# Attention in two-step blocks, one pool for all PSUM banks, and a new order of a linear-attention and feed-forward kernel

## The chip, the cores and the metric

The kernel runs on one core of a Trainium2 chip. The metric is the time of one execution on the device in microseconds (us); the smaller, the better. A core has a matrix engine (TensorE, PE in the profile, with its weight loads as PEld), a vector engine (VectorE, DVE), a scalar engine (ScalarE, ACT), GpSimd (POOL) and SyncE (SP). Each runs its own queue of instructions in order, and waits on semaphores for the others. In this kernel TensorE's results go to PSUM, in eight banks of up to 128 x 512 values of 32 bit; VectorE and ScalarE read them there. Loads and stores are DMA transfers that POOL, SP and ACT issue.

## The reference

Two parts, one after the other. First, a linear attention with decay for 4 batches and 8 heads, 768 positions, head size 64. In blocks of positions it is

```python
intra = einsum('bhic,bhjc->bhij', qb, kb) * Dmask     # lam ** (i - j) for i >= j, else 0
intra = einsum('bhij,bhjd->bhid', intra, vb)
inter = einsum('bhid,bhde->bhie', qb * lam_pow, kv_state)
out[:, :, sl] = intra + inter
kv_state = lam_block * kv_state + einsum('bhsd,bhse->bhde', kb * rev_pow, vb)
```

Then the result, as 3072 tokens of 512 values, goes through two matrix products with ELU between them:

```python
h = x @ w_in                                          # 512 x 2048
g = where(h > 0, h, exp(min(h, 0)) - 1)
out = g @ w_out                                       # 2048 x 512
```

The kernel may work with another block length (it uses 128), because the state carries the rest.

## The kernel before, in words

A **step** is 128 positions of one batch, all eight heads: 24 steps, step `s` being chunk `s // 4` of batch `s % 4`. The state of a batch (`sbd`, two copies used in turn) goes from a step to the one four later. Steps 0 to 3 have no state yet, so for them the part with the state is left out.

The attention of one step is made of these helpers. `load_step` (L73) issues three loads on POOL, of k and q into `kq` and of v into `vt`, cast to 16 bit on the way. `att_TK`, `att_TQ` and `att_T` (L205 to L227) transpose k and q on TensorE into PSUM and copy them out, with ScalarE or VectorE as their last arguments say; `att_D` (L229) lets a DMA do it instead, issued on SP, from step 8 on. `att_V` (L236) makes three products on VectorE: q times the decay (`qs`), v times the decay (`vd`), the old state times the decay (`sd`). `att_S` (L281) multiplies k and q into two banks `psS` and then multiplies these by the decay mask into `P`, on VectorE (L297). `att_U` (L258) multiplies k and `vd` into `psU`, and VectorE adds `sd` to give the new state (L275, L279). `att_O` (L301) multiplies P and v, and qs and the state, into `psO` (L323, L331), and ScalarE copies that to `xt` (L336), the input of the feed-forward part.

The feed-forward part is cut into quarters. `mm1(s, u)` (L346) makes one bank `psH` of the first product; ScalarE takes its exponential `e` (L359) and its positive part `r` (L364; with `relu=1` VectorE makes r, L362). `finish_g` (L367) joins the oldest pending e and r to `g` on VectorE (L376). From step 4 on two steps share an `mm1`, so a pair has eight of them (u = 0 to 7), of 256 columns. `mm2(s, i)` (L383) adds a quarter of the second product into `psM`; after i = 3 ScalarE copies the bank (L403) and SP stores it (L404). The weights `wi` and `wo` come in four blocks of 512 KB each (as stored), also issued by POOL.

Nothing is scheduled by a planner: the order of the calls in the kernel is the order on every engine. It is a long list written out by hand (L416 to L517), in which attention and feed-forward of steps 0 to 3 are mixed, and then a loop over pairs (L521): p = 4, 6, ..., 22. In the loop the attention of step p + 2 stands ahead of u = 0 and that of p + 3 ahead of u = 4, each with the `att_S` of the step after it; each u has one `mm1` of the pair and one `mm2` taken from the list `late`, in which the two steps of the pair alternate. At the start, `warm` (L409) puts matmuls of zeros between the first pieces.

PSUM is split by tags: psT one bank, psM two, psU one, psS two, psH two. A tile waits until the tile that last held its bank has been read.

What sets the order of loads is POOL's list (L107 to L127), in which block 1 of `wi` comes first, then step 1, then blocks 0 and 2 and so on. Step 0 comes by SP and ACT as 32 bit (`k32`, `q32`, `v32`) and is cast by VectorE (L418, L420) and ScalarE (L427).

Of the kernel before, what the change touches and what calls it, by code (L numbers as in the profile page):

```python
# [11 lines left out]
ALU = mybir.AluOpType  # L12
# [3 lines left out]
def kernel(  # L16
# [23 lines left out]
    NBV = 5  # L40
    SEP = 2
# [66 lines left out]
    load_step(0)  # L108
    load_wi(1)
    load_step(1)  # L110
    clear(sbd[2][1])
    clear(sbd[1][1])
    load_wi(0)
    load_wi(2)
    load_step(2)
    load_wi(3)
    clear(sbd[3][0])
    load_step(3)
    clear(sbd[0][1])
    clear(sbd[2][0])  # L120
    load_wo(0)
# [3 lines left out]
    clear(sbd[1][0])  # L125
    clear(sbd[3][1])
    load_step(4)  # L127
# [48 lines left out]
    def mask_arg(hh):  # L176
        for hp in range(NHP):
            h = 2 * hp + hh
            nc.vector.scalar_tensor_tensor(
                out=mask[:, hh, hp, :], in0=ijf[:], scalar=loglam[:, h : h + 1],  # L180
                in1=negm[:], op0=ALU.mult, op1=ALU.add,
            )
# [15 lines left out]

    def copy(e, out, in_):
        if e:  # L200
            nc.scalar.copy(out=out, in_=in_)
        else:
            nc.vector.tensor_copy(out, in_)

    def att_TK(s, e=1):  # L205
        psK = ps.tile([128, NHP, 128], FP16, tag="psT", name=f"psK{s}")
        transposes(psK[:], s, 0)
        t = asb.tile([128, NHP, 128], FP16, tag="kT", bufs=3, name=f"kT{s}")
        st[s]["kT"] = t[:]
        copy(e, t[:], psK[:])  # L210

    def att_TQ(s, e=0):

        psQ = ps.tile([128, NHP, 128], FP16, tag="psM", bufs=2, name=f"psQ{s}")
        transposes(psQ[:], s, 1)
        t = asb.tile([128, NHP, 128], FP16, tag="qT", bufs=3, name=f"qT{s}")
        st[s]["qT"] = t[:]
        copy(e, t[:], psQ[:])

    def att_T(s, ke=1, qe=0):  # L220
        psT = ps.tile([128, 2, NHP, 128], FP16, tag="psT", name=f"psT{s}")
        transposes(psT[:, 0], s, 0)
        transposes(psT[:, 1], s, 1)
        for i, (n, e) in enumerate((("kT", ke), ("qT", qe))):
            t = asb.tile([128, NHP, 128], FP16, tag=n, bufs=3, name=f"{n}{s}")
# [3 lines left out]
    def att_D(s):  # L229
        t = asb.tile([128, 2 * NHP, 128], FP16, tag="kqT", bufs=3, name=f"kqT{s}")  # L230
# [5 lines left out]
    def att_V(s):  # L236
# [3 lines left out]
        if c:  # L240
            d["qs"] = asb.tile([128, NHP, 128], FP16, tag="qs", bufs=2, name=f"qs{s}")
# [3 lines left out]
        d["vd"] = asb.tile([128, H, 64], FP16, tag="vd", bufs=2, name=f"vd{s}")  # L245
# [5 lines left out]
        if c:  # L251
            d["sd"] = asb.tile([128, NHP, 128], FP32, tag="sd", bufs=2, name=f"sd{s}")
# [5 lines left out]
    def att_U(s):  # L258
# [4 lines left out]
        psU = ps.tile([128, NHP, 64], FP32, tag="psU", name=f"psU{s}")  # L263
# [7 lines left out]
        new = sbd[b][c % 2]  # L271
# [9 lines left out]
    def att_S(s):  # L281
# [3 lines left out]
            ps.tile([128, NHP, 128], FP32, tag="psS", bufs=2, name=f"psS{s}_{hh}")  # L285
            for hh in range(2)
# [8 lines left out]
        d["P"] = asb.tile([128, 2, NHP, 128], FP16, tag="P", bufs=2, name=f"P{s}")  # L295
        for hh in range(2):
            nc.vector.tensor_tensor(  # L297
                out=d["P"][:, hh], in0=psS[hh][:], in1=mask[:, hh], op=ALU.mult
            )

    def att_O(s):  # L301
# [5 lines left out]
        elif s % 2 == 0:  # L307

            xt[s] = asb.tile([128, NHP, 2 * L], FP16, tag="xt2", bufs=3, name=f"xt{s}")
        else:  # L310
            xt[s] = xt[s - 1]
        x = 0 if s < ONE else s % 2

        if s < SEP:
            psO = ps.tile([128, NHP, 128], FP32, tag="psM", bufs=2, name=f"psO{s}")
        elif s == B:
            psO = ps.tile([128, NHP, 128], FP32, tag="psU", name=f"psO{s}")
        else:
            psO = ps.tile([128, NHP, 128], FP32, tag="psT", name=f"psO{s}")
# [16 lines left out]
        nc.scalar.copy(out=xt[s][:, :, x * L : (x + 1) * L], in_=psO[:])  # L336
# [9 lines left out]
    def mm1(s, u, relu=0):  # L346
        w = 1 if s < ONE else 2
        nt = NQ // w
        psH = ps.tile([128, nt, w * L], FP32, tag="psH", bufs=2, name=f"psH{s}_{u}")
# [8 lines left out]
        e = msb.tile([128, nt, w * L], FP32, tag="e", bufs=4, name=f"e{s}_{u}")  # L358
        nc.scalar.activation(e[:], psH[:], AF.Exp)  # L359
        r = msb.tile([128, nt, w * L], FP16, tag="r", bufs=4, name=f"r{s}_{u}")  # L360
# [46 lines left out]
    warm_ps = ps.tile([128, 512], FP32, tag="psH", bufs=2, name="warm")  # L407
# [7 lines left out]

    warm(13)  # L416
    mask_arg(0)
    nc.vector.tensor_copy(kq[0][:, 1], q32[:])  # L418
    att_TQ(0)
    nc.vector.tensor_copy(kq[0][:, 0], k32[:])  # L420
    warm(4)
    mask_exp(0)
    att_TK(0)
    mask_arg(1)
    mask_exp(1)
    warm(3)
    nc.scalar.copy(out=vt[0][:], in_=v32[:])  # L427
    att_S(0)
    att_V(0)
    warm(4)  # L430
    att_O(0)
    att_TK(1)
    att_U(0)
    att_V(1)
    mm1(0, 1, 1)
    att_TQ(1, 1)
    finish_g()
    att_S(1)
    mm1(0, 0, 1)
    att_O(1)  # L440
    finish_g()
    mm1(0, 2)
    mm1(1, 1)
    att_TQ(2, 0)
    load_step(5)
    att_V(2)
    finish_g()
# [128 lines left out]
```

## Time and profile before

| | |
|---|---|
| runs, median (lowest to highest) | 218.79 us (218.54 to 219.06), 3 runs |
| the profiled execution's own time | 218.84 us |
| its span | 217.0 us |
| PE, DVE, ACT, POOL busy | 206.8, 152.5, 137.9, 70.8 us |
| DMA | 24.84 MB, 13.24 MB of it through POOL's queue |
| granted TensorE clock | 1.00 |

The span is what the profiler saw of the engines; the execution's own time has 1.84 us around it. "Busy" sums the time of an engine's instructions. A matmul that waits for its operands can count as busy, so that PE's share says little about how much it computes: `mm1` of a pair needs 0.87 us for 8 matmuls and `mm2` 0.86 us for 4 where they follow each other without a wait. In the chain of waits each row is a start, a duration and what ran or was waited for; it follows the work that ended last back to its cause. The windows give busy time in us and instructions (x) for PE, PEld, DVE, ACT and POOL, then granted clock, busy share of the DMA engines and GB/s.

### The profile page before, as it was taken

The page shows a single profiled execution, that of the slowest core. Times are in us where ns is not written, and L with a number is a line of the kernel's source. Part 1 is how long each engine was busy: PE and PEld are TensorE (multiplying, and loading weights), DVE is VectorE, ACT ScalarE, POOL GpSimd, SP SyncE. Part 2 cuts the span into 40 slices and gives each one's busy share as a digit, 9 for nine tenths or more (in the row PEclk, how much of TensorE's full clock was granted, in tenths as well). Part 3 has the DMA queues.
Part 4 walks back from the last instruction along what each step waited for, and adds up shares of the span by engine and source line. Part 5 has one row for each costly group of instructions (what it writes and reads, how often), then busy time and mean ns, then how long its engine had stood idle before and what let it go on. Part 6 is the DMA issues. An engine that isn't in the chain of part 4 may idle for free.

```text
span 217.0 us, 5089 instructions
## 1 busy us (share of the span) xinstructions
PE 206.8 (95%) x2072; PEld 138.9 (64%) x2072; DVE 152.5 (70%) x266; ACT 137.9 (64%) x263; POOL 70.8 (33%) x90
## 2 busy tenths in 40 slices
PE   7778699999999999999999999999999999999993
PEld 2368576765666766766676676676676666666651
DVE  4785983899878868868868778778775464533440
ACT  3737564956755765865855855855955955866851
POOL 8875833865341242242242242144000000000000
PEclk9999999999999999999999999999999999999999
DMA  4999999999995994996995993999680320200202
GB/s 102 193 200 181 183 206 176 154 211 141 164 198 38 128 182 31 135 165 42 139 171 37 147 169 26 152 172 69 105 112 0 76 73 2 100 0 0 100 0 97
DMA packets 99767, 24.84 MB, mean 114 GB/s; under 512 B 92448, under 2 KB 96800, under 8 KB 99744
## 3 DMA queue, kind: packets, MB, share of 16 engines
q0 software_dynamic: 75984, 13.24, 77.7%
q1 hardware_dynamic: 21536, 10.62, 21.4%
q10 hardware_dynamic: 2224, 0.66, 1.4%
q8 instruction: 16, 0.26, 0.5%
q14 instruction: 7, 0.06, 0.1%
HBM read 27.27 MB, written 6.29 MB: 155 GB/s over the span
## 4 chain that ended last, share of the span: by engine, by line
PE 79%; DMA 9%; DVE 8%; issue 1%; ACT 1%; POOL 0%; POOLq 0%
PE psM L388 36%; PE psH L353 34%; DMA vt<-in_v_dram 5%; DMA wi<-in_moe_w_in_dram 4%; PE psO L323 3%; PE psS L291 3%; DVE g L376 2%; DVE P L297 2%; PE psO L331 2%; DVE vd L246 1%; DVE sbd L275 1%; PE psU L267 1%; DVE qs L242 1%; DVE sd L253 1%; ACT r L364 1%
## 5 line engine op out<-in xcount | busy, mean ns | idle before, releaser
L353 PE MATMUL psH<-xt,wi 128*128 128x256 f16 (+1 forms) x896 | 96.0, 257 | 2.0 <-DVE r L362 1.8
L388 PE MATMUL psM<-wo,g 128*128 128x512 f16 x384 | 97.3, 380 | 0.4 <-DVE g L376 0.4
L376 DVE SCALAR_TENSOR_TENSOR g<-e,r 128x512 f16<-128x512 f32 x96 | 64.7, 689 | 45.8 <-ACT r L364 45.5
L359 ACT ACTIVATE e<-psH 128x512 f32<-128x512 f32 x96 | 57.6, 600 | 57.4 <-PE psH L353 56.6
L353 PEld LDWEIGHTS <-wi 128*128 128x128 f16 x896 | 77.6, 98 | 23.3 <-DMA wi<-in_moe_w_in_dram 1.8
L364 ACT ACTIVATE r<-psH 128x512 f16<-128x512 f32 x93 | 55.7, 598 | 0.0
L388 PEld LDWEIGHTS <-g 128*128 128x128 f16 x384 | 35.4, 98 | 29.3 <-DVE g L376 0.9
L77 POOL DMA_DIRECT2D kq<-in_k_dram x23 | 20.3, 884 | 67.1 <-PE psU L267 57.1
L297 DVE TENSOR_TENSOR P<-psS,mask 128x512 f16<-128x512 f32 x48 | 30.9, 685 | 1.6 <-PE psS L291 1.1
L79 POOL DMA_DIRECT2D vt<-in_v_dram x23 | 20.5, 893 | 7.4 <-DMA wi<-in_moe_w_in_dram 2.1
L78 POOL DMA_DIRECT2D kq<-in_q_dram x23 | 20.5, 893 | 2.6 <-DMA wo<-in_moe_w_out_dram 2.6
L336 ACT CAST xt<-psO 128x512 f16<-128x512 f32 x24 | 14.1, 587 | 8.2 <-PE psO L331 6.4
L323 PEld LDWEIGHTS <-vt 128*64 128x64 f16 x192 | 9.7, 109 | 9.7 <-issue 8.1
L403 ACT COPY o<-psM 128x512 f32<-128x512 f32 x23 | 13.8, 607 | 3.0 <-PE psM L388 3.0
L323 PE MATMUL psO<-P,vt 128*64 128x128 f16 x192 | 13.8, 225 | 0.9 <-DVE P L297 0.9
L246 DVE TENSOR_TENSOR vd<-vt,rev 128x512 f16<-128x512 f16 x19 | 13.0, 685 | 1.1 <-DMA vt<-in_v_dram 1.1
L275 DVE TENSOR_TENSOR sbd<-psU,sd 64x256 f16<-64x256 f32 x32 | 13.4, 418 | 0.5 <-issue 0.2
L331 PE MATMUL psO<-qs,sbd 128*64 128x128 f16 x160 | 11.1, 219 | 0.0
L242 DVE TENSOR_TENSOR qs<-kqT,powi 128x512 f16<-128x512 f16 x16 | 11.0, 685 | 0.0
L253 DVE TENSOR_TENSOR sd<-sbd,lamL 128x512 f32<-128x512 f16 x16 | 10.9, 684 | 0.0
L412 PE MATMUL warm<-zero 128*128 128x512 f16 x24 | 7.9, 481 | 1.2 <-DVE zero L130 1.2
L331 PEld LDWEIGHTS <-sbd 128*64 128x64 f16 x160 | 9.0, 110 | 0.0
(54 smaller groups left out, 79.9 us busy)
## 6 DMA issues: line engine op xcount, KB each, us to landing
out_dram<-o SPq DMA_DIRECT2D x23, 256.0 KB, 2.6
kq<-in_k_dram POOLq DMA_DIRECT2D x23, 128.0 KB, 4.5
kq<-in_q_dram POOLq DMA_DIRECT2D x23, 128.0 KB, 4.4
vt<-in_v_dram POOLq DMA_DIRECT2D x23, 128.0 KB, 4.4
wi<-in_moe_w_in_dram POOLq DMA_DIRECT2D x4, 512.0 KB, 9.9
wo<-in_moe_w_out_dram POOLq DMA_DIRECT2D x4, 512.0 KB, 13.2
q<-in_q_dram ACTq DMA_DIRECT2D x1, 256.0 KB, 4.7
k<-in_k_dram SPq DMA_DIRECT2D x1, 256.0 KB, 5.5
```

Source lines behind the costliest of these rows:

```text
L77: nc.gpsimd.dma_start(out=kq[s][:, 0], in_=rows_of(k, s))
L78: nc.gpsimd.dma_start(out=kq[s][:, 1], in_=rows_of(q, s))
L79: nc.gpsimd.dma_start(out=vt[s][:], in_=rows_of(v, s))
L275: nc.vector.tensor_tensor(out=new[p, :, p], in0=psU[p], in1=d["sd"][p, :, p], op=ALU.add)
L297: nc.vector.tensor_tensor(out=d["P"][:, hh], in0=psS[hh][:], in1=mask[:, hh], op=ALU.mult)
L323: nc.tensor.matmul(psO[p, hp, :], lhsT=vt[s][:, 2 * hp + hh, :], rhs=d["P"][:, hh, hp, :], start=True, stop=(c == 0), skip_group_check=True,)
L331: nc.tensor.matmul(psO[p, hp, :], lhsT=sbd[b][(c - 1) % 2][:, hp, p], rhs=d["qs"][:, hp, :], start=False, stop=True, skip_group_check=True,)
L353: nc.tensor.matmul(psH[:, j, :], lhsT=wi[n // NQ][:, kk, n % NQ * 128 : (n % NQ + 1) * 128], rhs=xt[s][:, kk, :], start=(kk == 0), stop=(k ...
L359: nc.scalar.activation(e[:], psH[:], AF.Exp)
L364: nc.scalar.activation(r[:], psH[:], AF.Relu)
L376: nc.vector.scalar_tensor_tensor(out=t[:], in0=e[:], scalar=-1.0, in1=r[:], op0=ALU.add, op1=ALU.min)
L388: nc.tensor.matmul(acc[:], lhsT=g[s, i * NQ + n], rhs=wo[i][:, n, :], start=(i == 0 and n == 0), stop=(i == NWB - 1 and n == NQ - 1),)
```

## The change

- All tiles in PSUM come from one tag with eight banks (`bank`); which bank a tile gets follows from the order in which earlier ones are released.
- `att_S`, `att_U` and `att_O` are cut in two: the matmuls, and the work of VectorE or ScalarE on their results (`att_P`, `att_A`, `att_X`), so that the two can stand at different places. Two steps may share one bank for psU.
- In the loop the attention of two steps stands in one block at the start of a round: O and U of both, then S and P of the two steps after them (in the first round S and P stand ahead of u = 4). `mm2` works on the pair before the current one, one step at a time: four quarters of a step, then four of the next. The loop starts at p = 6.
- The hand-written part has another order. The attention of steps 0 to 3 comes ahead of nearly all of the feed-forward work. Loads are in another order too: k, q and v of steps 1 to 3 (all but one) stand ahead of the first weight block, which is block 0. Casts of k and q of step 0 move to ScalarE, both copies of step 4's transposes and one copy to `xt` to VectorE, and five `mm1` instead of three have r made by VectorE. There are 36 warm-up matmuls instead of 24, and the clears of state tiles are placed differently.
- Buffers: kq and vt six instead of five, e and r six instead of four, kT, qT, kqT four instead of three, qs, vd, sd, P four instead of two.

```diff
-    NBV = 5
-    SEP = 2
+    NBV = 6
...
-    def load_step(s):
+    def load_k(s):
         kq[s] = inp.tile([128, 2, H, 64], FP16, tag="kq", bufs=NBV, name=f"kq{s}")
+        if s:
+            nc.gpsimd.dma_start(out=kq[s][:, 0], in_=rows_of(k, s))
+
+    def load_q(s):
+        nc.gpsimd.dma_start(out=kq[s][:, 1], in_=rows_of(q, s))
+
+    def load_v(s):
         vt[s] = inp.tile([128, H, 64], FP16, tag="vt", bufs=NBV, name=f"vt{s}")
         if s:
-            nc.gpsimd.dma_start(out=kq[s][:, 0], in_=rows_of(k, s))
-            nc.gpsimd.dma_start(out=kq[s][:, 1], in_=rows_of(q, s))
             nc.gpsimd.dma_start(out=vt[s][:], in_=rows_of(v, s))
+
+    def load_step(s):
+        load_k(s)
+        load_q(s)
+        load_v(s)
...
-    load_step(0)
+    load_k(0)
+    load_v(0)
+    clear(sbd[1][0])
+    load_k(1)
+    load_q(1)
+    clear(sbd[0][1])
+    load_k(2)
+    load_q(2)
+    load_v(2)
+    load_k(3)
+    clear(sbd[2][0])
+    load_q(3)
+    load_v(1)
+    load_wi(0)
+    clear(sbd[2][1])
+    load_v(3)
     load_wi(1)
+    load_wi(2)
     clear(sbd[1][1])
+    clear(sbd[3][0])
+    load_wo(0)
     load_wi(3)
+    clear(sbd[3][1])
+    load_step(4)
     load_wo(1)
     load_wo(2)
     load_wo(3)
...
+    def bank(shape, dtype, name):
+        return ps.tile(shape, dtype, tag="bank", bufs=8, name=name)
+
...
-        psK = ps.tile([128, NHP, 128], FP16, tag="psT", name=f"psK{s}")
+        psK = bank([128, NHP, 128], FP16, f"psK{s}")
...
-        psQ = ps.tile([128, NHP, 128], FP16, tag="psM", bufs=2, name=f"psQ{s}")
+        psQ = bank([128, NHP, 128], FP16, f"psQ{s}")
...
-        psT = ps.tile([128, 2, NHP, 128], FP16, tag="psT", name=f"psT{s}")
+        psT = bank([128, 2, NHP, 128], FP16, f"psT{s}")
...
-    def att_U(s):
+    def att_U(s, pair=False):
...
-        psU = ps.tile([128, NHP, 64], FP32, tag="psU", name=f"psU{s}")
+        if pair and s % 2:
+            psU = st[s - 1]["psU2"][:, 1]
+        else:
+            d["psU2"] = bank([128, 2, NHP, 64], FP32, f"psU{s}")
+            psU = d["psU2"][:, 0]
...
-        new = sbd[b][c % 2]
+        d["psU"] = psU
+
+    def att_A(s):
+
+        c, b = divmod(s, B)
+        if c == NCH - 1:
+            return
+        d = st[s]
+        psU, new = d["psU"], sbd[b][c % 2]
...
-            ps.tile([128, NHP, 128], FP32, tag="psS", bufs=2, name=f"psS{s}_{hh}")
-            for hh in range(2)
+            bank([128, NHP, 128], FP32, f"psS{s}_{hh}") for hh in range(2)
...
-        d["P"] = asb.tile([128, 2, NHP, 128], FP16, tag="P", bufs=2, name=f"P{s}")
-        for hh in range(2):
-            nc.vector.tensor_tensor(
-                out=d["P"][:, hh], in0=psS[hh][:], in1=mask[:, hh], op=ALU.mult
-            )
+        d["psS"] = psS
+
+    def att_P(s, hh):
+        d = st[s]
+        if hh == 0:
+            d["P"] = asb.tile([128, 2, NHP, 128], FP16, tag="P", bufs=4, name=f"P{s}")
+        nc.vector.tensor_tensor(
+            out=d["P"][:, hh], in0=d["psS"][hh][:], in1=mask[:, hh], op=ALU.mult
+        )
...
-        elif s % 2 == 0:
+        elif xt[s] is None:
 
             xt[s] = asb.tile([128, NHP, 2 * L], FP16, tag="xt2", bufs=3, name=f"xt{s}")
-        else:
-            xt[s] = xt[s - 1]
-        x = 0 if s < ONE else s % 2
-
-        if s < SEP:
-            psO = ps.tile([128, NHP, 128], FP32, tag="psM", bufs=2, name=f"psO{s}")
-        elif s == B:
-            psO = ps.tile([128, NHP, 128], FP32, tag="psU", name=f"psO{s}")
-        else:
-            psO = ps.tile([128, NHP, 128], FP32, tag="psT", name=f"psO{s}")
+            xt[s ^ 1] = xt[s]
+        psO = bank([128, NHP, 128], FP32, f"psO{s}")
...
-        nc.scalar.copy(out=xt[s][:, :, x * L : (x + 1) * L], in_=psO[:])
+        d["psO"] = psO
+
+    def att_X(s, e=1):
+        x = 0 if s < ONE else s % 2
+        copy(e, xt[s][:, :, x * L : (x + 1) * L], st[s]["psO"][:])
...
-        psH = ps.tile([128, nt, w * L], FP32, tag="psH", bufs=2, name=f"psH{s}_{u}")
+        psH = bank([128, nt, w * L], FP32, f"psH{s}_{u}")
...
-            psM[s] = ps.tile([128, DM], FP32, tag="psM", bufs=2, name=f"psM{s}")
+            psM[s] = bank([128, DM], FP32, f"psM{s}")
...
+    def cast(e, part, x32):
+        copy(e, vt[0][:] if part == 2 else kq[0][:, part], x32[:])
+
...
     warm(13)
+    mask_arg(0, 3)
+    cast(1, 0, k32)
+    mask_arg(1, 2)
+    mask_arg(1, 3)
+    cast(1, 1, q32)
+    warm(5)
+    att_TQ(0, 1)
+    cast(1, 2, v32)
+    mask_arg(1, 0)
+    mask_arg(1, 1)
+    att_TK(1, 1)
     warm(4)
+    mask_arg(0, 1)
+    mask_arg(0, 0)
+    att_V(0)
+    att_TK(0, 0)
+    att_TQ(1, 0)
+    mask_arg(0, 2)
+    warm(4)
+    att_TQ(2, 0)
+    att_S(0)
+    att_V(2)
+    att_S(1)
+    warm(3)
+    mask_exp(1)
     mask_exp(0)
+    att_TK(2, 1)
     warm(3)
+    att_P(0, 0)
+    att_S(2)
+    att_T(3, 1, 1)
+    att_P(0, 1)
+    att_U(2)
+    att_P(2, 0)
     warm(4)
     att_O(0)
+    att_P(1, 0)
+    att_X(0, 1)
+    att_P(2, 1)
+    att_S(3)
+    att_P(1, 1)
+    att_O(2)
+    att_O(1)
+    att_X(2, 1)
+    att_X(1, 1)
+    att_P(3, 0)
+    att_P(3, 1)
+    att_V(1)
     att_U(0)
+    mm1(0, 0)
+    mm1(2, 0)
+    att_U(1)
+    att_V(3)
+    att_A(1)
     load_step(5)
     finish_g()
     powi_exp()
     att_U(3)
+    att_O(3)
+    att_X(3, 1)
+    finish_g()
+    mm1(1, 0)
+    finish_g()
+    att_A(0)
+    mm1(1, 1)
+    mm1(2, 1, 1)
+    mm1(0, 1, 1)
+    load_step(8)
+    att_A(2)
+    mm1(3, 0, 1)
+    finish_g()
+    mm1(1, 2)
+    finish_g()
+    mm1(0, 2, 1)
+    mm2(0, 0)
+    mm2(1, 0)
+    mm1(3, 1, 1)
+    mm2(2, 0)
+    att_A(3)
+    finish_g()
+    finish_g()
+    finish_g()
+    finish_g()
+    mm1(2, 2)
+    att_T(4, 0, 0)
+    finish_g()
+    finish_g()
+    mm1(3, 2)
+    finish_g()
+    mm1(2, 3)
+    finish_g()
+    mm1(0, 3)
     att_V(4)
     mm2(2, 1)
     load_step(7)
+    mm1(3, 3)
+    finish_g()
+    mm2(0, 1)
+    att_S(4)
+    load_step(9)
+    mm2(3, 0)
+    finish_g()
+    mm1(1, 3)
+    att_D(8)
+    mm2(3, 1)
+    att_P(4, 0)
+    att_P(4, 1)
+    finish_g()
+    mm2(3, 2)
+    mm2(3, 3)
+    att_T(5, 0, 1)
+    mm2(0, 2)
+    mm2(2, 2)
     att_V(5)
     att_O(4)
+    att_S(5)
+    att_X(4, 1)
+    att_U(5)
+    att_P(5, 0)
+    att_U(4)
+    att_P(5, 1)
+    att_D(9)
+    mm2(0, 3)
+    mm2(1, 1)
+    att_A(5)
+    att_T(7, 1, 1)
+    att_O(5)
+    att_A(4)
+    load_step(6)
+    att_X(5, 0)
+    mm2(1, 2)
+    att_V(7)
+    mm1(4, 1)
+    att_S(7)
+    mm1(4, 3)
+    att_P(7, 0)
+    att_P(7, 1)
+    mm1(4, 0)
+    finish_g()
+    finish_g()
+    mm2(2, 3)
+    att_T(6, 1, 1)
+    att_V(8)
+    mm2(1, 3)
+    mm1(4, 4)
+    finish_g()
     att_S(6)
     att_V(6)
+    att_S(8)
+    att_P(8, 0)
+    att_P(8, 1)
+    mm1(4, 2)
+    mm1(4, 5)
+    att_P(6, 0)
+    mm1(4, 6)
+    att_O(7)
+    load_step(10)
+    att_D(10)
+    load_step(11)
+    att_P(6, 1)
+    att_X(7, 1)
+    att_S(9)
+    mm1(4, 7)
+    att_U(7)
+    att_U(6)
+    att_P(9, 0)
+    att_P(9, 1)
+    att_O(6)
+    att_V(9)
+    att_D(11)
+    finish_g()
+    finish_g()
+    att_A(6)
+    finish_g()
+    finish_g()
+    load_step(12)
+    finish_g()
+    att_X(6, 1)
+    att_A(7)
+    load_step(13)
+    late = [(s, i) for s in (ONE, ONE + 1) for i in range(NWB)]
...
+    for p in range(ONE + 2, NSTEP, 2):
+        late += [(p + h, i) for h in range(2) for i in range(NWB)]
+        now = [s for s in (p + 2, p + 3) if s < NSTEP]
+        nxt = [s for s in (p + 4, p + 5) if s < NSTEP]
+        for s in now:
+            att_O(s)
+            att_X(s)
+            att_U(s, True)
+        at = 0 if p > ONE + 2 else NWB
...
         for u in range(2 * NWB):
-            s, j = p + 2 + u // NWB, u % NWB
-            if j == 0 and s < NSTEP:
-                att_O(s)
-                att_U(s)
-                if s + 1 < NSTEP:
-                    att_S(s + 1)
-            m2 = (p, u) not in ((ONE, 2), (NSTEP - 2, 3), (NSTEP - 2, 7))
-            if m2 and j == 0:
-                mm2(*late.pop(0))
+            if u == at:
+                for s in nxt:
+                    att_S(s)
+                    att_P(s, 0)
+                    att_P(s, 1)
+            if u == 0:
+                for s in now:
+                    att_A(s)
+            mm2(*late.pop(0))
             mm1(p, u)
-            if m2 and j:
-                mm2(*late.pop(0))
-            if j == 1 and s + 1 < NSTEP:
-                att_V(s + 1)
-            finish_g()
-            if s < NSTEP:
-                if j == 0 and s + 4 < NSTEP:
-                    load_step(s + 4)
-                if j == 1 and s + 3 < NSTEP:
-                    att_D(s + 3)
+            if u - at in (1, 2) and nxt:
+                att_V(nxt[u - at - 1])
+            if u:
+                finish_g()
+            if u < 2 and p + 8 + u < NSTEP:
+                load_step(p + 8 + u)
+            if u in (2, 3) and p + 4 + u < NSTEP:
+                att_D(p + 4 + u)
+        finish_g()
     while late:
         mm2(*late.pop(0))
 
```

(Left out: the changed numbers of SBUF buffers, the old hand-written list, and `mask_arg`, which now makes one head's mask.)

More of the change, by code (lines that the diff above doesn't have):

```diff
@@ L174, with mask_arg @@
     mask = cpool.tile([128, 2, NHP, 128], FP32, name="mask")
[L176 to L181, printed above, removed]
-            )
+    def mask_arg(hh, hp):
+        h = 2 * hp + hh
+        nc.vector.scalar_tensor_tensor(
+            out=mask[:, hh, hp, :], in0=ijf[:], scalar=loglam[:, h : h + 1],
+            in1=negm[:], op0=ALU.mult, op1=ALU.add,
+        )
     def mask_exp(hh):
@@ L229, in att_D @@
     def att_D(s):
[L230 removed]
+        t = asb.tile([128, 2 * NHP, 128], FP16, tag="kqT", bufs=4, name=f"kqT{s}")
         nc.sync.dma_start_transpose(
@@ L244, in att_V @@
             return
-        d["vd"] = asb.tile([128, H, 64], FP16, tag="vd", bufs=2, name=f"vd{s}")
+        d["vd"] = asb.tile([128, H, 64], FP16, tag="vd", bufs=4, name=f"vd{s}")
         nc.vector.tensor_tensor(
@@ L404, in mm2 @@
                 nc.sync.dma_start(out=out[r0 : r0 + L, :], in_=o[:])
-    warm_ps = ps.tile([128, 512], FP32, tag="psH", bufs=2, name="warm")
+    warm_ps = bank([128, 512], FP32, "warm")
     def warm(n):
@@ L481 @@
     att_U(3)
-    att_T(4, 1, 1)
+    att_O(3)
[19 more added lines that the diff above has]
+    att_A(3)
     finish_g()
     finish_g()
-    att_V(4)
-    mm2(1, 3)
-    load_step(6)
-    mm2(0, 3)
+    finish_g()
+    finish_g()
+    mm1(2, 2)
@@ L489 @@
+    att_T(4, 0, 0)
+    finish_g()
+    finish_g()
     mm1(3, 2)
     finish_g()
-    att_T(5, 1, 1)
-    att_S(4)
-    att_U(4)
-    mm1(3, 0)
-    mm2(2, 0)
+    mm1(2, 3)
+    finish_g()
+    mm1(0, 3)
+    att_V(4)
     mm2(2, 1)
     load_step(7)
+    mm1(3, 3)
     finish_g()
-    att_T(6, 1, 1)
-    att_S(5)
+    mm2(0, 1)
[10 more added lines that the diff above has]
+    mm2(3, 2)
@@ L501 @@
+    mm2(3, 3)
+    att_T(5, 0, 1)
+    mm2(0, 2)
+    mm2(2, 2)
     att_V(5)
     att_O(4)
-    mm2(2, 2)
-    mm1(3, 3)
+    att_S(5)
[23 more added lines that the diff above has]
+    finish_g()
```

96 lines of the change are left out of this document (8 added, 88 removed).

## The prediction

> **What bounds the kernel now.** I read the page first: busy shares and slices.
>
> ```profile
> span 217.0 us, 5089 instructions
> PE 206.8 (95%) x2072; PEld 138.9 (64%) x2072; DVE 152.5 (70%) x266; ACT 137.9 (64%) x263; POOL 70.8 (33%) x90
> ...
> DVE  4785983899878868868868778778775464533440
> ```
>
> TensorE looks busy throughout, but a matmul that waits counts as busy, and VectorE stands at 8 and 9 in the slices from 25 to 60 us. So I read the busy time by stage next.
>
> ```profile
> 15.00:20.00 5.00, 4.33 (x76) 3.80 (x71) 3.44 (x7) 2.58 (x5) 3.77 (x6) 1.00 1.84 181
> 20.00:25.00 5.00, 3.24 (x57) 2.90 (x55) 3.92 (x8) 2.78 (x7) 3.36 (x6) 1.00 1.85 180
> ...
> 80.00:100.00 20.00, 20.00 (x189) 13.57 (x188) 16.13 (x28) 13.26 (x27) 5.47 (x7) 1.00 1.21 111
> ```
>
> Up to 25 us TensorE (first figure) has holes, and the granted clock is 1.00 all the same. Last the chain of waits (start, us, what).
>
> ```profile
> 1.48 8.37 DMA wi<-in_moe_w_in_dram
> ...
> 10.13 11.15 DMA vt<-in_v_dram
> ...
> 46.23 0.57 issue
> 46.80 0.68 DVE P L297
> 47.48 0.60 DVE qs L242
> 48.08 0.60 DVE vd L246
> 48.68 0.60 DVE sd L253
> ...
> 60.42 0.18 PE psO L323 x2
> 60.60 0.06 PE psO L331 x2
> ...
> 60.99 0.12 PE psU L267 x8
> 61.12 0.33 PE psS L291 x8
> 61.45 0.97 PE psM L388 x4
> 62.42 1.75 PE psH L353 x16
> 64.16 0.86 PE psM L388 x4
> ```
>
> Three stages: loads until 21.3 us; VectorE for nearly all of 42.7 to 59.8; then TensorE alone, dense, until its last matmul ends at 213.35. Check of "dense": at 61.45 there remain 76 first-matmul quarters (`mm1`, 0.87 each), 79 second-matmul quarters (`mm2`, 0.862) and attention of 17.45: 66.1 + 68.1 + 17.45 = 151.7, and 61.45 + 151.7 = 213.1.
>
> **The rounds.** A step's attention costs TensorE 1.14: psO 0.58, psU 0.12, psS 0.33, and 0.11 on the next psM. The first psO pair takes 0.18 where others take 0.06, psS 0.33 where its eight in four side-by-side pairs need 0.22, the first psM 0.97 against 0.86. So entering psO, going from psU to psS, and leaving each cost about 0.115; psO to psU costs nothing. A two-step block O,U,O,U,S,S pays these three once: 2 × 1.14 − 0.34 = 1.94. This is the change's gain per round, hidden by nothing, because TensorE ends these rounds.
>
> Do the new waits give it back? I walked one round from the block's start. `mm1`'s last tile leaves ScalarE at 1.1, its g VectorE at 1.85; then four P (4 × 0.65) to 4.5, four state adds (0.42) to 6.2, three att_V products, a g, three more: 10.7; g's catch up by 13. The banks as the built kernel assigns them: `mm1` u=2 waits for the first P (2.6, needed at about 6.3), u=3 and 4 and the second psM for the other P's, u=6 for the adds (6.2, needed at 13), the first psM for the last relu (1.1, needed at 1.8). All early. VectorE needs 18 × 0.62 + 1.7 = 12.9 of 15.8. With `mm2` a round behind, its g's are long done. Cost: zero, covered by at least 0.7 (first psM); if that cover goes, the loss is per round.
>
> **The front.** Nine 128 KB loads and four 512 KB blocks were issued by wo0; the DMA view, one issue at a time, gives landings in order: wi1 9.85, wi0 14.9, wi2 17.4, wo0 28.4, wo1 31.1, k5 40.0, q5 40.9, v5 41.8: about 0.88 a load and 2.5 a block. Now eight loads go ahead of the first block, which lands at 9.85 + 8 × 0.88 = 16.9 instead of 9.85; then v3 17.8, wi1 20.3, wi2 22.8, wo0 25.3, wi3 27.8, step 4 by 30.5, wo1 33, wo2 35.5, wo3 38, step 5 by 41, steps 8, 7, 9, 6 at 2.64 each, by 51.5. GpSimd issues the eight at 0.89 each, from 2.05 to 10.2 with two clears of 0.5 between; faster than they drain. Before this: k1 8.2, q2 10.9, v2 11.8, v1 14.4.
>
> Attention: ScalarE is free at 7.4, casts k and q there (0.49 apart; before on VectorE, 0.79 and 0.61), copies qT0 by 9.6 and kT1 by 10.6; S0 at 11.5. VectorE waits for v2, makes vd2 by 12.9, then six P to 16.9; O1 follows by 17.4, U0, and `mm1(0,0)` at 17.6 (before: 12.6). Weights have 0.7 to spare there, and 0.8, 1.8 and 1.1 at wi1, wi2 and wo0.
>
> From 17.6 to O of step 8, TensorE has 16 × 0.89 + 8 × 0.87 + 16 × 0.862 = 35.0 of feed-forward; attention 5.9 (T 0.44, O 0.46, U 0.12, S 0.22 each); some 20 switches, 2.3. So O8 at 60.8. VectorE has two idle places, before v2 and from 21.8 to 23.35, where it waits for the r of `mm1(1,0)` behind powi. From there to step 9's products: 17 g and 5 relu at 0.62, 18 products at 0.60, 12 P at 0.65, 10 half adds at 0.42, three transposed copies at 0.42, one xt copy 0.65: 38.3, so 61.7; with waits for T7's and T6's ScalarE copies 62.7. (The two extra relus, both T4 copies and the xt5 copy, moved from ScalarE, are counted.) O9 needs qs9 at 61.5 and U9 vd9 at 62.1: 0.5 of stall. The chain of before also holds 0.57 and 0.46 that I could not have foreseen, in 17 us; over 38 us that is 2.3. Most were P waiting for psS, which I place here, so I take 1.2, between 0 and 2.3. SP's transposes of steps 8 and 9 wait for loads (43, 48.5) with output stores queued behind; four output buffers cover that, and psS8 comes at 55. T6 has 1.5 over its load; a later load is a stall.
>
> **Sum.** Left at O8: 72 × 0.87 + 80 × 0.862 = 131.6, and attention 2.05 (step pair 8, S apart) + 5 × 1.94 + 1.70 (no U) + 1.15 (O alone) = 14.6: 146.2. Then 3.65 from the last matmul to the end of the span, as before: copy and store are the same. 60.8 + 0.5 + 1.2 + 146.2 + 3.65 = 212.35. The profiled execution took 218.84 with a span of 217.0, so 1.84 around it: 214.2. It is 0.05 above the median 218.79. Gain 4.6: 2.7 switches, the rest a fuller front.
>
> **Rivals.**
> *Front slips a little.* Loads at 1.0 instead of 0.88, or VectorE waits at 2.3 and more: each load counts eightfold before wi0 (+1.0, less 0.7 of slack) and further for wo blocks. +1.5 to +3.4: 215.7 to 217.6. For: v2 landed 1.9 after q2 once. Against: all other spacings.
> *The slow side: small loads drain badly without blocks between them.* Place: the eight ahead of wi0. At 1.9 each (v2's row) wi0 lands at 25, 7.4 past need: 221.6. It decides from 1.54 a load (4.6 + 0.7 over eight, on 0.88). Against: steps 4 and 5, six in a row, took 0.8 to 1.2.
> *Round stalls.* One pool lets an accumulator or state bank hold up `mm1`; nine rounds, 0.5 each cancels the gain: 216.5 to 220, about half of it slower. For: VectorE at 12.9 of 15.8 in bursts. Against: the walk.
> *The clock drops in the front.* TensorE in 13 to 17.6 has short pieces with waits between. First 13 warm-up matmuls took 0.385 each, 0.216 is the later pace; a stretch of 3.4 us of work at the slow pace costs 2.6: 216.8. Against: 1.00 at 3.24 busy of 5.
> The Trainium skill (TensorE: Matmul & The Clock Gate, "A second HAM failure mode: psum-queue depth-cycling") says that cycling through PSUM banks can idle TensorE often enough to make its clock swing; by it one pool would cost this in any stage. No row of this trace shows such a swing, so it weighs little.
> *The change does nothing*: switches cost what they did (another unseen wait takes 2.7) and the later `mm1` start eats the front: 218.8.
>
> **How the numbers follow.** As summed 0.58 (211.9 to 215.7: waits 0 to 2.3, plus 0.4 of rounding); front slip 0.16; clock 0.04; round stalls 0.10, half and half; slow loads 0.09; nothing 0.03. Range 211.9 to 217.6, which holds 0.58 + 0.16 + 0.04 and a third of the round stalls: 0.81. Three runs spread by 0.24%, so 0.2% is about what can be told from no change. Faster 0.58 + 0.16 + 0.04 + 0.05 = 0.83, same 0.03, slower 0.09 + 0.05 = 0.14.
>
> **What would show it.** wi0 landing near 17 and first psH near 17.6; VectorE back to back from 23 to 62; step 8's psO near 61 to 63; later rounds of 15.8 (before 16.15) with psO, psU in pairs; granted clock 1.00. Wrong: first psH after 20, psH idle for P or sbd in the rounds, or rounds still at 16.1.

## The result and the profile after

The changed kernel takes 216.94 us (median of 8 runs), the kernel before 218.92 (8 runs): a ratio of 0.9898, 95% interval 0.9862 to 0.9934. Run again beside the experiments below it took 216.93 (6 runs, 215.60 to 217.44) against 218.44 (17 runs): 0.9914, interval 0.9881 to 0.9947. So it is faster by about 1%, 2.0 and 1.5 us; the forecast was 214.2, 4.6 us faster. It lies inside the range given (211.9 to 217.6), but less than half of the forecast gain came.

Executions more than 1.5% above the fastest of their kernel are left out of the ratios: one of the eight here (744 us, with a matmul of 512 columns in 1105 ns instead of 379 at a recorded clock of 1.00), and below two of the twelve with loads held back and three of the twelve with psS of step 11 alone later. The profile read here is of an ordinary execution of the changed kernel, 217.07 us with a span of 215.3.

The page: its first line, the line of busy time, and VectorE in 40 slices.

```profile
span 215.3 us, 5135 instructions
...
PE 204.9 (95%) x2084; PEld 139.1 (65%) x2084; DVE 154.3 (72%) x269; ACT 136.5 (63%) x260; POOL 70.6 (33%) x90
...
DVE  5589789989999999947968958959649442344410
```

VectorE is now nearly full from 24 to 91 us, as planned, but TensorE's share is 95%, as before. The busy time by stage (columns: window, length, TensorE, weight load, VectorE, ScalarE, GpSimd with their counts, granted clock, DMA share, GB/s) says where the holes are now:

```profile
15.00:20.00 5.00, 5.00 (x108) 3.85 (x107) 4.72 (x8) 3.81 (x8) 4.87 (x7) 1.00 1.44 198
20.00:25.00 5.00, 4.98 (x99) 4.72 (x94) 3.47 (x7) 5.00 (x14) 1.21 (x2) 1.00 1.24 206
...
68.00:72.00 4.00, 2.62 (x26) 1.64 (x23) 3.87 (x9) 2.65 (x5) 3.45 (x4) 1.00 2.51 164
72.00:76.00 4.00, 3.65 (x31) 2.44 (x32) 4.00 (x7) 1.08 (x2) 0.87 (x1) 1.00 2.83 148
...
80.00:84.00 4.00, 2.86 (x69) 2.04 (x64) 3.34 (x6) 1.89 (x4) 3.20 (x4) 1.00 1.89 199
```

The holes of the front are closed (5.00 and 4.98 of 5, before 4.33 and 3.24). New ones stand at 68 to 76 and 80 to 84 us, in a stretch where the kernel before had TensorE without a gap:

```profile
68.00:72.00 4.00, 4.00 (x55) 2.78 (x54) 2.88 (x6) 1.94 (x5) 2.50 (x3) 1.00 0.33 24
72.00:76.00 4.00, 4.00 (x30) 2.63 (x28) 3.48 (x6) 3.76 (x8) 0.13 (x1) 1.00 1.48 156
```

The chain of waits of the changed kernel (start, us, what) names what the holes are:

```profile
51.70 12.72 DMA kq<-in_q_dram
...
64.47 7.84 DMA kqT<-kq
...
72.35 0.40 PE psS L320 x8
...
73.84 8.65 DMA kqT<-kq
...
82.54 0.40 PE psS L320 x8
```

And the waits of TensorE from 30 to 212 us (what it waited for: total, times, longest):

```profile
PE psS L320 <- DMA kqT<-kq: 2.9, 2, 1.7
PE psT L208 <- DMA kq<-in_q_dram: 0.3, 1, 0.3
```

Twice TensorE stands still for a transpose by DMA (`att_D`, issued by SyncE): 1.74 us ahead of psS of step 11, 1.14 ahead of psS of step 13. Together 2.88 us; the result misses the forecast by 2.7. From 82.94 on all is dense until the last matmul ends at 211.60.

### The profile page after: what moved, and what is told of

The parts are those of the page before. It is cut to its first block, busy times and chain, and to the rows that moved or that the text cites. A ratio compares the mean times of both kernels' runs of the same rounds, so it can differ in the third digit from the quotient of the medians.

```text
span 742.3 us, 5135 instructions
## 1 busy us (share of the span) xinstructions
PE 737.4 (99%) x2084; PEld 337.0 (45%) x2084; DVE 158.2 (21%) x269; ACT 141.9 (19%) x260; POOL 70.7 (10%) x90
## 4 chain that ended last, share of the span: by engine, by line
PE 99%; DVE 0%; ACT 0%; issue 0%
PE psM L417 43%; PE psH L382 42%; PE warm L441 4%; PE psO L348 3%; PE psS L320 3%; PE psO L356 2%; PE psT L208 1%; PE psU L289 1%; PE psQ L208 0%; PE psK L208 0%; DVE o L428 0%; ACT o L427 0%; DVE zero L146 0%
## 5 line engine op out<-in xcount | busy, mean ns | idle before, releaser
L417 PE MATMUL psM<-wo,g 128*128 128x512 f16 x384 | 337.1, 1105 | 0.0
L382 PE MATMUL psH<-xt,wi 128*128 128x256 f16 (+1 forms) x896 | 336.6, 628 | 0.0
L382 PEld LDWEIGHTS <-wi 128*128 128x128 f16 x896 | 188.2, 220 | 191.4 <-issue 184.4
L417 PEld LDWEIGHTS <-g 128*128 128x128 f16 x384 | 79.7, 211 | 158.7 <-issue 155.1
L330 DVE TENSOR_TENSOR P<-psS,mask 128x512 f16<-128x512 f32 x48 | 30.1, 684 | 61.8 <-PE psS L320 61.8
L348 PE MATMUL psO<-P,vt 128*64 128x128 f16 x192 | 35.6, 425 | 0.0
L356 PE MATMUL psO<-qs,sbd 128*64 128x128 f16 x160 | 33.6, 449 | 0.0
L441 PE MATMUL warm<-zero 128*128 128x512 f16 x36 | 30.7, 1098 | 1.2 <-DVE zero L146 1.2
L348 PEld LDWEIGHTS <-vt 128*64 128x64 f16 x192 | 21.8, 181 | 11.3 <-issue 10.5
L356 PEld LDWEIGHTS <-sbd 128*64 128x64 f16 x160 | 21.8, 195 | 0.5
L320 PE MATMUL psS<-kqT 64*128 64x128 f16 x128 | 13.8, 430 | 0.0
```

The lines of the kernel that those rows point to most:

```text
L320: nc.tensor.matmul(psS[hh][:, hp, :], lhsT=d["kT"][p, hp, :], rhs=d["qT"][p, hp, :], start=True, stop=True, skip_group_check=True,)
L330: nc.vector.tensor_tensor(out=d["P"][:, hh], in0=d["psS"][hh][:], in1=mask[:, hh], op=ALU.mult)
L348: nc.tensor.matmul(psO[p, hp, :], lhsT=vt[s][:, 2 * hp + hh, :], rhs=d["P"][:, hh, hp, :], start=True, stop=(c == 0), skip_group_check=True,)
L356: nc.tensor.matmul(psO[p, hp, :], lhsT=sbd[b][(c - 1) % 2][:, hp, p], rhs=d["qs"][:, hp, :], start=False, stop=True, skip_group_check=True,)
L382: nc.tensor.matmul(psH[:, j, :], lhsT=wi[n // NQ][:, kk, n % NQ * 128 : (n % NQ + 1) * 128], rhs=xt[s][:, kk, :], start=(kk == 0), stop=(k ...
L417: nc.tensor.matmul(acc[:], lhsT=g[s, i * NQ + n], rhs=wo[i][:, n, :], start=(i == 0 and n == 0), stop=(i == NWB - 1 and n == NQ - 1),)
```

## The experiments

The first two expectations were written before this trace was read; their theories are waits in the front (A), a clock that drops (B) and rounds that spare nothing (C). In the third and fourth, theory A is the reading above: rounds and front come as forecast, and the missing gain sits in these two waits; its rival B is that behind the waits something else ends the stretch anyway. All kernels below are compared with the kernel before, run beside them on the same chip, where it took 218.32 to 218.55; us are medians of all runs. A profile is of one execution.

| kernel | us | runs, lowest to highest | TensorE's waits for kqT in its profile |
|---|---|---|---|
| changed kernel, again | 216.93 | 6, 215.60 to 217.44 | 1.74 + 1.14 |
| split rounds | 217.14 | 12, 216.56 to 218.18 | 1.00 |
| psS of 11 and 13 later | **214.11** | 4, 214.04 to 214.41 | none |
| 11 and 13 transposed by TensorE | 216.31 | 5, 216.07 to 216.69 | none (1.4 for a copy) |
| loads 14, 15 held back | 217.74 | 12, 216.09 to 220.56 | 1.45 + 2.33 |
| eight load buffers | 218.47 | 12, 216.94 to 219.55 | 2.45 + 0.15 + 0.42 |
| psS of 11 later alone | 216.09 | 12, 215.11 to 219.46 | 1.45 |
| psS of 10 and 11 later | 215.12 | 6, 215.00 to 215.48 | none (1.03 for VectorE) |
| psS later, split rounds from step 12 | 216.04 | 6, 215.90 to 216.71 | none |

### The changed kernel again, and split rounds

> The changed kernel once more, for a profile in which TensorE runs at its usual pace. Theory A (the walk of the prediction was right in the rounds, and about 2.5 us were lost in the front by waits): time 216 to 217.5, granted clock 1.00 in every stage, first psH near 17.6, step 8's psO at 63.5 to 65, rounds of 15.8. Theory B (the clock drops in the front, where TensorE has only short pieces): a stretch before 30 us with a granted clock under 1 in the slices and first-step psH groups of 16 taking clearly over 0.89, rounds of 15.8, and executions that differ by more than 0.5%. Theory C (the rounds gained nothing): rounds of 16.1.

It gave the profile above, and that leaves none of the three as it was put: psH starts on time, the clock is 1.00, and the rounds take 15.81 us. The waits are behind the front.

The split kernel puts one step's psO, psU, psS ahead of the first quarter of a round and the other's ahead of the fifth, from the second round on; the front is untouched.

```diff
-        for s in now:
-            att_O(s)
-            att_X(s)
-            att_U(s, True)
...
+            elif u % NWB == 0:
+                if u // NWB < len(now):
+                    att_O(now[u // NWB])
+                    att_X(now[u // NWB])
+                    att_U(now[u // NWB])
+                if u // NWB < len(nxt):
+                    att_S(nxt[u // NWB])
```

> The changed kernel with the rounds from p = 8 on as before: one step's psO, psU, psS ahead of u = 0 and the other's ahead of u = 4; the front and all else as changed. If a switch between the forms of matmul costs 0.115 each and the blocks of two steps spare three a round: rounds of 16.15 and a time 2.3 us over the changed kernel (six rounds of 0.34, and 0.3 in the two short ones). If the gain came from the front alone: the same time as the changed kernel within 0.5 us.

Measured: 217.14, ratio to before 0.9945 (0.9926 to 0.9963), only 0.2 above the changed kernel. By the time alone the blocks are worth nothing. The chain of waits says otherwise. First the changed kernel, one round from its first psM to the next, then the split one, half a round each:

```profile
82.94 0.97 PE psM L417 x4
...
98.75 0.97 PE psM L417 x4
```

```profile
79.63 0.97 PE psM L417 x4
...
87.70 0.97 PE psM L417 x4
...
95.77 0.97 PE psM L417 x4
```

15.81 us against 16.14: the price of the switches is there, 0.33 a round. But the split kernel asks for psS of step 13 four quarters later, so that wait is gone, and the one for step 11 is 1.00 instead of 1.74: 1.9 less waiting, about what five rounds with psU (0.33 each) and two without (0.23) lose, 2.1. One edit moved two costs against each other; the experiment was badly chosen, and a cleaner one follows at the end.

### psS of steps 11 and 13 two quarters later

Only the order changes; loads and transposes stay.

```diff
-            if u == at:
-                for s in nxt:
+            for j, s in enumerate(nxt):
+                if u == at + {0: (0, 2), 1: (0, 2)}.get((p - ONE - 2) // 2, (0, 0))[j]:
                     att_S(s)
                     att_P(s, 0)
                     att_P(s, 1)
...
-            if u - at in (1, 2) and nxt:
-                att_V(nxt[u - at - 1])
+            for j, s in enumerate(nxt):
+                if u == at + {0: (1, 3), 1: (1, 3)}.get((p - ONE - 2) // 2, (1, 2))[j]:
+                    att_V(s)
```

> Only the order of the attention work changes: psS of step 11 stands two quarters (3.5 us) after psS of step 10, and psS of step 13 two quarters after psS of step 12, with their masked products and att_V two quarters later too; all loads and transposes as in the changed kernel. Theory A (the missing gain sits in two waits of TensorE for transposed kq of steps 11 and 13, 1.74 and 1.14 us idle, about 3.05 with the pieces around them): both waits are gone, two more switches of matmul form at about 0.23 each come in, so 2.6 us less than the changed kernel, near 214.3. Theory B (behind these waits something else ends the stretch, VectorE's products or the granted clock that differs from run to run): the time stays within 0.5 us of the changed kernel.

Measured: 214.11 (214.04 to 214.41), ratio to before 0.9797 (0.9767 to 0.9828); 2.8 less than the changed kernel, expected 2.6. Its busy time by stage, same columns:

```profile
68.00:72.00 4.00, 4.00 (x34) 2.52 (x33) 3.90 (x8) 2.65 (x5) 3.06 (x5) 1.00 2.16 158
72.00:76.00 4.00, 4.00 (x35) 2.52 (x33) 4.00 (x8) 2.22 (x5) 0.56 (x1) 1.00 1.66 197
...
80.00:84.00 4.00, 4.00 (x34) 2.50 (x32) 3.93 (x9) 1.95 (x4) 3.89 (x5) 1.00 1.74 198
```

The holes are closed and nothing takes their place; VectorE is as full as before and ends nothing. This settles where the gain went. It is also the fastest of all the versions.

### Why the transposes are late

Four runs ask what makes them so. In the first, steps 11 and 13 are transposed by TensorE:

```diff
-    att_D(11)
...
             mm1(p, u)
+            if p == ONE + 2 and u in (3, 7):
+                att_T(11 if u == 3 else 13, 1, 1)
...
-            if u in (2, 3) and p + 4 + u < NSTEP:
+            if u in (2, 3) and p + 4 + u < NSTEP and p + 4 + u != 13:
                 att_D(p + 4 + u)
```

> Steps 11 and 13 are transposed by TensorE with two ScalarE copies each, a quarter before psS of their pair, instead of by DMA from SyncE; all else as in the changed kernel. Theory A: the waits for kqT of steps 11 and 13 go (about -3.05), eight transposes and their switches come in for each (0.44 + 0.23, twice: +1.3), so 1.7 us less than the changed kernel, near 215.2; the transposes by DMA that are left land in less than the 7.8 to 8.7 us of the changed kernel, since fewer of them share the DMA engines. Theory B: +1.3 us, near 218.2.

Measured: 216.31. The waits for kqT are gone, but psS of step 11 now waits for the second ScalarE copy of the transposes:

```profile
PE psS L320 <- ACT qT L220: 1.4, 1, 1.4
```

One wait of 1.4 us that I had not put into the sum more than covers the 1.1 between 216.3 and the 215.2 expected. Of the DMA transposes that are left, step 14's lands in 3.1 us (6.5 in the changed kernel), step 10's in 6.3 (7.0) and step 12's in 7.6 (7.7). In the changed kernel step 14's was issued at 80.2, before step 13's had landed (82.5), so a transpose ahead on the same queue may account for part of the delay; but step 12's is as slow with none ahead of it, and what is left beside it then is loads and stores.

In the second, the loads of steps 14 and 15 wait for a late g tile:

```diff
+            if p == ONE + 2:
+                if u == 6:
+                    hold = cpool.tile([128, 1], FP16, name="hold")
+                    nc.gpsimd.tensor_copy(hold[:], g[6, 10][:, 0:1])
+                    load_step(14)
+                    load_step(15)
-            if u < 2 and p + 8 + u < NSTEP:
+            elif u < 2 and p + 8 + u < NSTEP:
                 load_step(p + 8 + u)
```

> The loads of steps 14 and 15, which are not needed before about 97 us, are held back from 67-74 us to about 78 us (GpSimd copies one element of the g tile of the first round's sixth quarter before it issues them); all else as in the changed kernel. Theory A1 (the transposes of steps 11 to 13 are late because loads of later steps share the DMA engines with them): kqT of step 13 lands in 5 us or less instead of 8.65, its wait of 1.14 us on TensorE is gone and that of step 11 (1.74) is smaller: 1.2 to 2.0 us less than the changed kernel, near 215.3. Theory A2 (the transposes are slow by themselves, several in a row behind one late load): kqT lands as late as before, no change beyond 0.3 us.

Measured: 217.74 (217.34 for the ten runs that enter the ratio), no faster than the changed kernel: the ratio to before has the interval 0.9910 to 0.9966, the changed kernel's 0.9881 to 0.9947. TensorE's psS with its waits (start, us, and in brackets the idle time and what ended it):

```profile
72.37 0.40 PE L320 MATMUL psS<-kqT 64*128 64x128 f16 x8 [1.45 <-DMA kqT<-kq]
81.02 0.62 PE L320 MATMUL psS<-kqT 64*128 64x128 f16 x16
...
99.57 0.40 PE L320 MATMUL psS<-kqT 64*128 64x128 f16 x8 [2.33 <-DMA kqT<-kq]
```

The part on step 13 came true: its transpose lands 4.2 us after its issue instead of 8.65 (the chain above), and steps 12 and 13 stand in one piece at 81.02 without a wait.

```profile
L249 SPq DMA_TRANSPOSE kqT<-kq x1: 1241/1241/1241, 73.7 to 73.7; - x1
DMA to landing us min/median/max: 4.2/4.2/4.2
```

That shows the crowding for step 13: the same transpose, issued 0.15 earlier, with the six loads out of its way, takes half as long. It doesn't show it for step 11, the larger of the two waits: that transpose, issued at 64.3 while the loads of steps 12 and 13 were under way as before, lands in 8.0 us (7.84), and no run took those loads alone away. But the held loads went out from 80.8 us on (I had expected 78), straight ahead of those of steps 16 and 17, twelve in a row, and now the transpose of step 15 meets them: it lands in 9.7 us and costs 2.33. The crowd was moved, not dissolved.

The third gives loads more buffers:

```diff
-    NBV = 6
+    NBV = 8
```

> Eight instead of six buffers for the loads of a step (NBV = 8), so that loads of steps 12 and 13 no longer wait for the state products of steps 7 and 6 at 61.8 us; all else as in the changed kernel. Theory A1 (crowded DMA engines): the loads 12 to 15 come earlier, step 13's wait of 1.14 us goes, but step 11's transposes meet more loads, so its wait stays or grows by up to 2 us: between 1.2 us less and 1 us more than the changed kernel, likeliest 0.5 less. Theory A3 (only late buffers make the loads and with them the transposes late): both waits go, about 3 us less, near 214.

Measured: 218.47, as slow as before (ratio 0.9991, interval 0.9967 to 1.0015). The loads did start earlier (step 12's at 53.9 us instead of 61.8), and the wait for step 11 grew while three transposes now keep TensorE waiting:

```profile
72.62 0.40 PE L320 MATMUL psS<-kqT 64*128 64x128 f16 x8 [2.45 <-DMA kqT<-kq]
...
81.82 0.40 PE L320 MATMUL psS<-kqT 64*128 64x128 f16 x8 [0.15 <-DMA kqT<-kq]
...
98.23 0.40 PE L320 MATMUL psS<-kqT 64*128 64x128 f16 x8 [0.42 <-DMA kqT<-kq]
```

So the lack of buffers is not the cause. Loads that run further ahead meet more of the transposes: in this execution those of steps 14 and 15 land after 8.7 and 8.5 us (6.5 and 3.4 in the changed kernel). The waits in this profile are close to the changed kernel's, the median is 1.5 us above it: the profiled execution was the fastest of twelve, and what the others waited for is not known.

The fourth puts off step 11's psS alone; against the kernel with both later:

```diff
-                if u == at + {0: (0, 2), 1: (0, 2)}.get((p - ONE - 2) // 2, (0, 0))[j]:
+                if u == at + {0: (0, 2), 1: (0, 0)}.get((p - ONE - 2) // 2, (0, 0))[j]:
```

> As the changed kernel, with psS of step 11 alone two quarters (3.5 us) later; psS of step 13 stays beside that of step 12. Theory A4 (the two waits are one wall: the DMA engines deliver kqT of step 13 at about 81 to 82.5 us whatever TensorE does, so that what the first wait no longer costs the second one takes): the wait for step 13 grows from 1.14 to about 2.3 us, and the time is within 0.8 us of the changed kernel's 216.9, likeliest 216.3. Theory A5 (the two waits are separate and add): 1.74 less, one more switch of 0.23, so 215.4.

Measured: 216.09, where 216.3 was expected of one wall and 215.4 of two waits that add. The wait for step 13 is now

```profile
80.99 0.40 PE L320 MATMUL psS<-kqT 64*128 64x128 f16 x8 [1.45 <-DMA kqT<-kq]
```

Here TensorE is ready at 79.5, 1.9 earlier than in the changed kernel (81.4), and the transpose lands at 81.0, 1.5 earlier (82.5); so of the first wait most stays saved in this one execution, more than the wall theory allowed. The twelve runs spread from 215.1 to 219.5, and the nine that enter the ratio have a median of 215.66, nearer to two waits; the spread is too wide to tell 215.4 from 216.3. Whether the second wait is a fixed wall stays open; that it remains, and grows a little, is seen.

### Both psS of the first round later

> As the kernel with both psS later (214.11 us), but psS of step 10 waits for that of step 11, so that both stand in one piece two quarters later and one switch in and out of the form of psS is spared. If the switches cost what the rounds show, 0.23 less: 213.9, nothing else changes; if the later products of step 10 reach VectorE too close to their use in the next block, up to 0.7 more, shown by psO of step 10 waiting for P or qs.

```diff
-                if u == at + {0: (0, 2), 1: (0, 2)}.get((p - ONE - 2) // 2, (0, 0))[j]:
+                if u == at + {0: (2, 2), 1: (0, 2)}.get((p - ONE - 2) // 2, (0, 0))[j]:
```

Measured: 215.12, one us above the 214.11. It is the second branch of the expectation, but dearer than its 0.7, and it is step 11's psO that waits, not step 10's. TensorE and VectorE around it:

```profile
79.67 0.25 PE L356 MATMUL psO<-qs,sbd 128*64 128x128 f16 x2 [1.03 <-DVE qs L260]
```

```profile
74.12 2.48 DVE L330 TENSOR_TENSOR P<-psS,mask 128x512 f16<-128x512 f32 x4 [0.25 <-PE psS L320]
...
78.92 0.69 DVE L260 TENSOR_TENSOR qs<-kqT,powi 128x512 f16<-128x512 f16 x1
```

Four P, step 10's three products and a g, back to back, bring step 11's qs to 79.6, and psO needs it 1.03 earlier. With the switch spared this makes 0.8 of the one us. It is a wait for VectorE's products, not for a bank, and it is met only when psS comes this late.

### Split rounds without the waits

With both psS later, the rounds from step 12 on are split as above; nothing else ends them now.

```diff
+        if p <= ONE + 4:
+            for s in now:
+                att_O(s)
+                att_X(s)
+                att_U(s, True)
...
+            elif u % NWB == 0:
+                if u // NWB < len(now):
+                    att_O(now[u // NWB])
```

> As the kernel with both psS later (214.11 us), but from the third round (step 12) on one step's psO, psU, psS stands ahead of the first quarter and the other's ahead of the fifth, as in the kernel before. With the waits for transposes out of the way this shows the price of the two-step blocks alone. Theory R1 (each switch of matmul form costs about 0.115): four rounds with psU lose 0.33 each, the two after them 0.23 each, 1.8 in all: 215.9. Theory R2 (the rounds spare nothing, the gain is all the front's): 214.1, within 0.4.

Measured: 216.04 (215.90 to 216.71), 1.9 above the 214.11, expected 1.8. The two-step blocks are worth what the forecast said, and this holds in the time, not only in the trace.

## Why the prediction was right, and where it was wrong

The forecast gain was 4.6 us, and 2.0 came (1.5 in the second measurement). The step that failed is the one from the front to the rounds: the sum goes from psO of step 8 straight to rounds in which TensorE waits for nothing, and so puts at zero, without a reason, the waits for the transposed inputs of steps 10 to 13. The runs showed 2.9 us of such waits (1.74 and 1.14).

**Right: the rounds.** Forecast 15.8 a round instead of 16.15; measured 15.81 (82.94 to 98.75), and 1.9 us for six rounds when they are split again. The terms were three switches at 0.115, read off the first pieces of psO, psS and psM. The Trainium skill (TensorEngine Tiling (Array Packing), "Key Properties") says that changing the tiling mode drains TensorE; the runs agree: the three switches between matmul forms that a block of two steps spares cost 0.33, and going from psO to psU, both in tiles of 128*64, costs nothing. The new waits that the pool could bring into a round cost zero, as forecast: after 83 us TensorE waits for nothing.

**Right: the front.** First psH at 17.82 (forecast 17.6), VectorE nearly back to back from 24 to 70 with qs and vd of step 9 begun at 61.5 and 62.1 (the forecast had them ready at these times, 0.6 earlier, and psO and psU of step 9 wait for neither), psO of step 8 at 61.9 (forecast 60.8 + 0.5 + 1.2 = 62.5). The granted clock is 1.00 in every stage shown, but that figure alone doesn't settle it: it is 1.00 in the kernel before from 0 to 5 us too, where the first warm-up matmuls took 0.385 each instead of 0.216. The pace does: the first nine groups of 16 for psH take 0.95 each where the forecast had 0.89, far from such a factor of 1.8, so the clock rival fell for this execution. The swings that the Trainium skill (TensorE: Matmul & The Clock Gate, "A second HAM failure mode: psum-queue depth-cycling") warns of are not in this trace. Of the 1.7 set down for waits there (1.2 unforeseen, 0.5 for step 9's products) TensorE shows about 0.6: 0.27 for wo0, which landed at 27.1 instead of 25.3, and 0.32 for step 6's load.

**Right: what is left after O8.** Forecast 146.2; measured 211.60 - 61.9 = 149.7, of which 2.88 are the two waits: 146.8. The end behind the last matmul took 3.70 (forecast 3.65), and 1.77 lie around the span (1.84).

**Wrong: the stretch between the front and the steady rounds.** The words "all early" held for the banks that they spoke of, and psS of step 8, put at 55, came at 56.3 without a wait. But having walked SP's transposes for steps 8 and 9 only, I closed the count at O8 and took the rest from one steady round. Between the front and the steady rounds lie the transposes of steps 10 to 13, and no sentence of the prediction has them. Two sizes are wrong there.

First the loads. I gave each 0.88 to the end; the landing times of the loads hold this until q of step 9 at 49.0, but nine loads later, q of step 11 lands at 64.4: 1.7 each, while four output stores and the transposes of steps 8 and 9 are under way. Loads 8, 7, 9 and 6 were to be there by 51.5; the last came at 55.9, and step 6's transposes waited 0.32 for one although I had counted 1.5 to spare.

Second the landing of a transpose. What the view of this tile says of the time from issue to landing, the kernel before first, then the changed one:

```profile
DMA to landing us min/median/max: 3.0/3.5/7.2
```

```profile
DMA to landing us min/median/max: 3.0/4.9/9.6
```

The prediction has no duration for it. The median of before, 3.5, is that of the steady rounds; the maximum, 7.2, belongs to the first transpose at 53.7 us, the one that lay among the loads, and this view would have shown it. In the changed kernel the transposes of steps 8 to 13 land after 9.4, 9.6, 7.0, 7.8, 7.7 and 8.7 us, step 15's in 3.4. With 3.5 instead of 7.84 and 8.65 neither wait would exist, by the trace's own issue times (64.47 + 3.5 and 73.84 + 3.5, ahead of TensorE's need at 70.6 and 81.4).

What crowds them is shown for step 13 by the held loads, 4.2 instead of 8.65; for step 11 it is argued from that. The Trainium skill (DMA: Bandwidth & Descriptors, "Queues, rings and completion order") says that each DMA engine takes turns between the queue rows that have work, a packet at a time. By that a transpose on SP's queue gets only a share while GpSimd's loads are pending; 8.65 against 4.2 agrees with it, though no run here shows the turns themselves.

So the mechanisms that the sum has were right, and a term was missing: +2.9 us of waits for the transposes of steps 11 and 13. The proof is the kernel with these two psS later: 214.11, where the sum without that term gave 214.2, its last matmul ending at 201.69 + 6.92 = 208.6 (forecast 62.5 + 146.2 = 208.7). That it fits to 0.1 is partly luck: this kernel pays two more switches (0.46) that the sum doesn't have, and fewer waits in the front than the sum allowed.

**The rivals.** Two of them hold the measured 216.9, and neither for its reason. "Front slips a little" (215.7 to 217.6) spoke of the loads ahead of the weights and of VectorE's waits; the weights cost 0.27, and it was later loads that came late. "Round stalls" (216.5 to 220) spoke of a bank or a state that holds up `mm1` in every round; what held TensorE up were transposed inputs, twice. So it is luck that the time lies inside the range.

## What to carry to other kernels

When a change makes the front denser, walk every consumer's inputs until the steady state is reached, not only until the front's last piece; the steps in between have the latest loads and the fullest queues. Take a transfer's duration from the row that had the same company on the DMA engines, not from the median of a quiet stage. And when a consumer waits for a crowded transfer, ordering the consumer later (two quarters here, 2.8 us) can be cheaper than moving the loads, which in two tries here (earlier with more buffers, later by holding them back) only crowded other transfers.

## What was not expected of the hardware

- **More room made it slower.** Eight load buffers instead of six cost 1.5 us (218.47 against 216.93, while the kernel before took 218.55 and 218.44 beside them). The one profile of it doesn't show where.
- **Kernels that wait for these transposes scatter, it seems.** Those without such a wait spread by 0.4 to 0.8 us over their runs, those with one by 1.6 to 4.5 (table above); but they also have fewer runs, 4 to 6 against 6 to 12, and the kernel before, without such waits, spreads by 2.6 over 23. In four of these five kernels some of the longer runs have a mean granted clock of 0.984 to 0.992, which no run of the four kernels without such a wait shows; but the kernel before has 0.982 and 0.983 in two of those 23 runs (220.55 and 219.98), and runs at 1.00 differ by 2.2 us too (loads held back: 216.09 and 218.28), so the clock is not all of it, and which causes which was not tried.
